# Agent attention and a squared-ReLU MLP on one core: 128- and 64-row spreads, and the weave on two engines

## The chip, the core and the metric

The kernel runs on one core of a Trainium2 chip. TensorE (PE) multiplies matrices into PSUM, VectorE (DVE), ScalarE (ACT) and GpSimd (POOL) do elementwise work, and SyncE (SP) issues the transfers, which 16 DMA engines carry out. The metric is device time in microseconds (us), the median of several runs. The profile comes from one execution of its own.

## The reference

Four batches of 12480 queries attend to 49 agents, which have attended to 12480 keys and values before. The result goes token by token through an MLP of width 2048 with a squared ReLU. All is computed to float32 accuracy.

```python
def sm(a, b):
    s = scale * (a @ b.transpose(0, 2, 1))
    e = np.exp(s - s.max(-1, keepdims=True))
    return e / (e.sum(-1, keepdims=True) + 1e-09)
agent_v = sm(agents, k) @ v          # per batch, 49 x 128
x = (sm(q, agents) @ agent_v).reshape(B * N, 128)
h = np.maximum(x @ w_in, 0.0)
out = (h * h) @ w_out
```

## The kernel before

The kernel never forms x. It folds `agent_v @ w_in` into one 49-row weight per batch (`w_hi` and `w_lo`, a high and a low part in the type fp32r), so that the first MLP matmul takes the 49 softmax probabilities of a token as its input. For accuracy the probabilities too are split in two parts, high and low.

**Steps.** The 49920 tokens are cut into tiles of 512, and the 2048 hidden columns into 8 pairs of 128. A step is one tile and one pair: `mm1` (L432, 6 matmuls into `h`), `relu` on ScalarE (L438), and for two steps together `square` on ScalarE (L441), `high` (L445) and `low` (L449) on VectorE, which make `gh` and `gl`. Five steps later (`LAG`) `mm2` (L460, 12 matmuls) takes them into an output pair, which `store` sends out every eighth step. A block s is 1024 tokens, 16 steps; there are 48.75 blocks. PSUM holds two `h` tiles.

**Probabilities of a block.** `mm1` reads block s from two tiles: `p_a` has the high parts in partitions 0 to 48 and the low parts in 64 to 112, `p_b` the other way round. For blocks 0 to 2 they are made with matmuls. For s > 2 the way is this: scores (L179), `q_shift`, `q_exp`, `q_inverse`, then `q_norm` on GpSimd (L349), `q_hi` on ScalarE (L353), `q_lo` on GpSimd (L356). `q_words` (L375, GpSimd, two calls) takes the 32-bit parts apart into 16-bit words in the single tile `words`, whose columns 49 to 63 and 113 to 127 stay zero. `q_turn` (L380, SyncE) transposes `words` into `turned` with a DMA. `q_weave` (L384, ScalarE) puts lower and upper 16-bit words together again in `woven`, a full tile of 128 partitions. `q_spread` (L391, SyncE) copies `woven` into `p_b` in two transfers of 49 rows, halves exchanged, and into `p_a` in one of 113 rows (`AW` = 64 + 49). A row is 1024 float32 values, 4 KB.

**Batch work.** For batches 1 to 3 keys and values are loaded in 13 pieces each (`kt`, `vt`; L174, L221), scored (L179), reduced, made into exponentials (`sk`; GpSimd L214, ScalarE L217) and multiplied with v (L229), woven in between the steps of the batch before.

**What sets the order.** The program is written out by hand in an order that a planner makes: `at(t, f)` gives a function a place in units of steps, and `chain` finds free places on the engines with the distances of the table `hop` (two steps from GpSimd or PE to ScalarE, for instance). Each engine goes through its own instructions in this order. Loads of `kt`, `vt` and `qt` stand 5 steps ahead of their matmuls. All transfers go through SyncE's one queue, so one that waits holds up the next. `plan_tokens` sets the turn 1.9 steps after the words, the weave 5 steps (and the half of a place that `chain` adds) after them, and the spread 0.9 steps after the weave, at least 3 steps before the block's first `mm1`:

```python
at(end + 1.9, q_turn, s)
_, end = chain(end + 5, [("ACT", q_weave, s)])
at(end + .9, q_spread, s)
```

Of the kernel before, what the change touches and what calls it, by code (L numbers as in the profile page):

```python
# [13 lines left out]
U16 = mybir.dt.uint16  # L14
# [4 lines left out]
P = 128  # L19
CH = 120  # L20
G = 8
# [4 lines left out]
def agent_attention_relu2_kernel(ctx: ExitStack, tc: tile.TileContext, qT, kT, v, agT, w_in, w_out, outT):  # L26
# [6 lines left out]
    nc = tc.nc  # L33
# [10 lines left out]
    AW = L + A  # L44
    rg = (slice(0, L), slice(L, P))
# [6 lines left out]
    ra = (slice(0, A), slice(L, AW))  # L52
# [3 lines left out]
    io = ctx.enter_context(tc.tile_pool(name="io", bufs=9))  # L56
# [98 lines left out]
    kts, vts, pss = {}, {}, {}  # L155
# [150 lines left out]
    PT, qs, es, sms, pps = {}, {}, {}, {}, {}  # L306
# [72 lines left out]
        pss["t", s] = io.tile([P, 2 * G, P], U16, name="turned", tag="io")  # L379
        nc.sync.dma_start(out=pss["t", s], in_=words.rearrange("p c w n -> p (c w n)"), transpose=True)  # L380

    def q_weave(s):
        PT["x"] = io.tile([P, G, P, 2], U16, name="woven", tag="io")
        nc.scalar.copy(PT["x"].rearrange("p c n w -> p c w n"), pss.pop(("t", s)).rearrange("p (c w) n -> p c w n", w=2))  # L384

    def q_spread(s):
        if s > 2:
            x = PT.pop("x").rearrange("p c n w -> p (c n w)").bitcast(F32).rearrange("p (c n) -> p c n", n=P)
            pa, pb = PT[s] = (wk.tile([P, G, P], F32R, name="p_a"), wk.tile([P, G, P], F32R, name="p_b"))
            for to, src in ((pb[ra[0]], x[ra[1]]), (pb[ra[1]], x[ra[0]]), (pa[:AW], x[:AW])):  # L390
                nc.sync.dma_start(out=to.bitcast(F32), in_=src)  # L391
            return
        pa, pb = PT[s]
        x = PT.pop("x") if s == 0 else None
        todo = ((pa[ra[0]], x[ra[0]]), (pb[ra[1]], x[ra[0]]), (pa[ra[1]], x[A:2 * A]), (pb[ra[0]], x[A:2 * A])) if s == 0 else (
            (pb[ra[0]], pa[A:2 * A]), (pb[ra[1]], pa[ra[0]]), (pa[ra[1]], pb[ra[0]]))
        for to, src in todo:
            nc.sync.dma_start(out=to.bitcast(F32), in_=src.bitcast(F32))
# [74 lines left out]
    def at(t, f, *args):  # L473
        steps.append((t, len(steps), f, args))
# [11 lines left out]
    def chain(t, todo):  # L486

        first = prev = None  # L490
        while todo:
            n = 1
            while todo[0][0] == "PE" and n < len(todo) and todo[n][1] in reads_bank and todo[n][0] != "PE":
                n += 1
            t += hop[prev][todo[0][0]] if prev else 0
            while True:
                g, p, ts = t, None, []
                for e, *_ in todo[:n]:
                    g += hop[p][e] if p else 0
                    while (e, g) in taken or (e == "PE" and g not in slots):  # L500
                        if p == "PE" and e == "DVE":
                            break
                        g += 1
                    ts.append(g)
                    p = e
                if todo[0][0] != "PE" or ts[-1] <= ts[0] + 1:
                    break
                t += 1
            for (e, f, *args), g in zip(todo, ts):
                soon = e == "DVE" and prev == "PE"  # L510
                if soon:
                    read.add(g)
                else:
                    taken.add((e, g))
                at(g + (.49 if soon and f is q_shift else .47 if soon else .45 if e == "PE" else .5), f, *args)
                prev = e
            first = ts[0] if first is None else first
            t, todo = ts[-1], todo[n:]
        return first, t
# [3 lines left out]
    def plan_tokens(s, base):  # L523
        todo = [("ACT", q_exp, s), ("DVE", q_inverse, s), ("POOL", q_norm, s), ("ACT", q_hi, s)]
        todo += [("POOL", q_lo, s), ("PE", q_transpose, s), ("ACT", q_copy, s)] if s < 3 else [
            ("POOL", q_words, s, 0), ("POOL", q_lo, s), ("POOL", q_words, s, 1)]
        if s > 1 and s % 2 == 0:
            m = min(2, NSG - s)
            first, base = chain(base, [("PE", q_scores, s, m), ("DVE", q_shift, s, m)])
            for x in range(s, s + m):  # L530
                at(first - 5, q_load, x)
            base += 3
        _, end = chain(base, todo)
        if s > 2:
            at(end + 1.9, q_turn, s)
            _, end = chain(end + 5, [("ACT", q_weave, s)])
        at(end + .9, q_spread, s)
        assert end + 3 < s * NF, (s, end)

    def plan_batch(b, base):  # L540

        end = b * N // TT * NJ
        for n in range(0, NS, 2):
            m = min(2, NS - n)
            first, t = chain(base + int(n * 4.6), [("PE", k_scores, b, n, m), ("ACT", k_copy, n, m), ("DVE", k_pmax, n, m)])
            for x in range(n, n + m):
                if b > 1 or x:
                    at(max(base - (6 if b > 1 else 0), first - 5), k_load, b, x)
            if n == NS - 3:
                chain(t + 1, [("DVE", k_max, 0, NS - 1)])  # L550
        _, t0 = chain(t + 1, [("DVE", k_max, 1)])
        _, t0 = chain(t0 + 4, [("PE", k_max, 2), ("DVE", k_max, 3)])
        _, t0 = chain(t0 + 3, [("PE", k_max, 4), ("DVE", k_max, 5)])
        done, d = {}, (end - 31 - t0) / NS
        for n in range(NS):
            _, done[n] = chain(t0 + 1 + int(n * d), [("POOL", k_sub, n), ("ACT", k_exp, n)])
            if n:
                _, y = chain(done[n] + 1, [("DVE", e_sum, n)])
            if n == NS - 1:
                _, y = chain(y + 1, [("DVE", a_last, 0)])  # L560
            if n % 2 or n == NS - 1:
                x = n - n % 2
                first, t = chain(done[n] + 2 if n % 2 else y + 4, [("PE", v_acc, x, n + 1 - x), ("DVE", v_sum, x)])
                for y in range(x, n + 1):
                    at(first - 5, v_load, b, y)
        at(first + .46, a_last, 1)
        at(t + .475, a_last, 2)
        _, e = chain(t + 2, [("PE", w_make_all, b, 0), ("ACT", w_make_all, b, 1), ("DVE", w_make_all, b, 2)])
        assert e + 2 < end, (e, end)
        return t + 1  # L570
# [29 lines left out]
    for n in range(NS):  # L600
        t = Z + 6.3 + 2.07 * n
# [38 lines left out]
    at(t0 + 9.7, q_copy, 0)  # L640
    at(t0 + 9.74, q_load, 1)
    at(t0 + 9.75, q_spread, 0)
    at(t0 + 9.76, hold, 0)
    at(t0 + 9.77, k_load, 1, 0)
    t = t0 + 13.4
# [22 lines left out]
    for y, x in enumerate((1.15, 1.16, 1.17)):  # L668
        at(x, w_first, 0, 4, 4, y, nc.vector)
    at(3.1, warm_rows, 6)  # L670
    plan_tokens(1, 3)
    for s in range(2, NSG):
        plan_tokens(s, (s - 2) * NF + NF // 2 + LAG - (3 if s > 2 and s % 2 == 0 else 0))
    t = 0
    for b in range(1, B):
        t = plan_batch(b, t)
# [41 lines left out]
```

## Time and profile before

| | us |
|---|---|
| median of 3 runs (2337.61 to 2344.29) | 2340.14 |
| the profiled execution | 2340.53 |
| its span, first to last instruction | 2338.8 |
| PE busy | 1929.4 |
| ACT busy | 1733.2 |
| DVE busy | 1640.9 |
| POOL busy | 327.4 |

Busy times of an engine leave out the time in which it waits. A busy PE need not run at full speed: the granted clock has two levels, 2.4 GHz (1.00) and 1.2 GHz (0.50), and a stretch shows a mean of them. The DMA share is the mean over the 16 DMA engines. A wait is put down to what ended last before it.

### The profile page before, as it was taken

Reading aid. Unit: us, or ns where it says so; the run is one execution under the profiler, and the core shown is the slowest. Engines: PE = TensorE matmul, PEld = TensorE weight load, DVE = VectorE, ACT = ScalarE, POOL = GpSimd, SP = SyncE. Lnnn points to the kernel's source line nnn. Section 1 sums busy time; section 2 is a strip of 40 time slices with the busy share of each in tenths; the row PEclk is TensorE's granted clock in tenths of the full one; section 3 lists DMA queues with packets and bytes.
Section 4 is the critical chain, followed back from the end, with each engine's and each line's share of the span. In section 5 each row is a group of like instructions: output and inputs, shape, how many; then the busy total and the mean of one; then the engine's idle time right before and its main releaser. Section 6 shows DMA issues by size and latency. Waiting matters only on the chain.

```text
span 2338.8 us, 51487 instructions
## 1 busy us (share of the span) xinstructions
PE 1929.4 (82%) x23244; PEld 1588.4 (68%) x23244; DVE 1640.9 (70%) x1274; ACT 1733.2 (74%) x1535; POOL 327.4 (14%) x244
## 2 busy tenths in 40 slices
PE   9998878788877788788886878879787887888788
PEld 7776766676756666577675766667666776676676
DVE  7886767776776677757676667767667677677676
ACT  5886777787766777778776777768776877787786
POOL 1111222111012121110101220111101101101100
PEclk9998999899988889989998899989889999899899
DMA  8231222322221222222231222212211211121110
GB/s 341 100 107 37 84 79 72 97 66 94 88 75 54 61 75 88 70 81 66 92 98 59 59 55 82 91 61 66 86 41 57 59 49 62 43 64 62 44 52 27
DMA packets 144298, 177.78 MB, mean 76 GB/s; under 512 B 100602, under 2 KB 100858, under 8 KB 144078
## 3 DMA queue, kind: packets, MB, share of 16 engines
q1 hardware_dynamic: 144078, 174.48, 24.3%
q8 instruction: 182, 2.98, 0.5%
q14 instruction: 38, 0.31, 0.0%
HBM read 83.02 MB, written 25.56 MB: 46 GB/s over the span
## 4 chain that ended last, share of the span: by engine, by line
DMA 45%; PE 35%; ACT 10%; issue 4%; SPq 4%; DVE 1%; POOL 1%; ACTq 0%; DVEq 0%
DMA p_a<-woven 30%; PE pair L460 19%; PE h L432 13%; DMA kt<-kT 7%; DMA vt<-v 7%; ACT woven L384 5%; ACT rg L438 4%; SPq L391 3%; PE pair L179 1%; PE pair L229 1%; ACT rg L441 1%; POOL words L375 0%; DMA raw<-w_in 0%; ACT ob L465 0%; PE pair L238 0%
## 5 line engine op out<-in xcount | busy, mean ns | idle before, releaser
L438 ACT ACTIVATE rg<-h 128x1024 f32<-128x1024 f32 (+1 forms) x784 | 790.1, 1020 | 561.9 <-PE h L432 560.6
L449 DVE TENSOR_TENSOR gl<-rg,gh 128x2048 fp32r<-128x2048 f32 x392 | 922.3, 2353 | 19.3 <-DVE gh L445 0.5
L445 DVE CAST gh<-rg 128x2048 fp32r<-128x2048 f32 x392 | 490.4, 1251 | 435.7 <-ACT rg L441 265.5
L441 ACT ACTIVATE rg<-rg 128x2048 f32<-128x2048 f32 x392 | 749.4, 1912 | 7.9
L432 PE MATMUL h<-p_a,w_hi 49*128 49x512 f32 (+4 forms) x1616 | 544.6, 413 | 247.8 <-DMA p_a<-woven 223.7
L460 PE MATMUL pair<-gh,wo_hi 64*128 64x512 f32 x3136 | 655.1, 403 | 0.2 <-issue 0.2
L460 PE MATMUL pair<-gh,wo_lo 64*128 64x512 f32 x3136 | 653.7, 402 | 0.1
L432 PE MATMUL h<-p_b,w_hi 49*128 49x512 f32 (+4 forms) x1616 | 529.4, 414 | 1.0 <-DMA p_b<-w_lo 1.0
L432 PEld LDWEIGHTS h<-p_a,w_hi 49*128 49x128 f32 x1616 | 303.5, 196 | 308.4 <-issue 237.3
L460 PE MATMUL pair<-gl,wo_hi 64*128 64x512 f32 x3136 | 509.2, 396 | 1.3 <-DVE gl L449 1.3
L460 PEld LDWEIGHTS pair<-gh,wo_lo 64*128 64x128 f32 x3136 | 328.2, 193 | 67.2 <-issue 0.8
L460 PEld LDWEIGHTS pair<-gh,wo_hi 64*128 64x128 f32 x3136 | 328.8, 194 | 61.3 <-issue 0.6
L460 PEld LDWEIGHTS pair<-gl,wo_hi 64*128 64x128 f32 x3136 | 319.3, 190 | 60.7 <-DVE gl L449 3.0
L432 PE MATMUL h<-p_a,w_lo 49*128 49x512 f32 (+4 forms) x808 | 326.0, 403 | 0.3 <-issue 0.3
L432 PE MATMUL h<-p_b,w_lo 49*128 49x512 f32 (+4 forms) x808 | 326.1, 404 | 0.0
L432 PEld LDWEIGHTS h<-p_b,w_hi 49*128 49x128 f32 x1616 | 298.8, 196 | 25.2 <-DMA p_b<-w_lo 1.3
L349 POOL TENSOR_TENSOR e<-e,sm 128x392 f32<-128x392 f32 x48 | 79.1, 1648 | 1342.5 <-DVE sm L346 1312.2
L375 POOL COPY words<-pp 128x784 uint16<-128x784 uint16 x92 | 123.6, 1343 | 524.9 <-ACT pp L353 522.0
L432 PEld LDWEIGHTS h<-p_a,w_lo 49*128 49x128 f32 x808 | 157.2, 194 | 25.8
L432 PEld LDWEIGHTS h<-p_b,w_lo 49*128 49x128 f32 x808 | 157.1, 194 | 5.7 <-issue 0.5
L384 ACT COPY woven<-turned 128x2048 uint16<-128x2048 uint16 x46 | 116.0, 2522 | 0.0
L229 PE MATMUL pair<-sk,vt 120*32 120x49 f32 x2496 | 41.2, 235 | 78.2 <-DMA vt<-v 78.2
(108 smaller groups left out, 884.8 us busy)
## 6 DMA issues: line engine op xcount, KB each, us to landing
vt<-v SPq DMA_DIRECT2D x52, 516.0 KB
qt<-qT SPq DMA_DIRECT2D x49, 512.0 KB
kt<-kT SPq DMA_DIRECT2D x52, 480.0 KB
outT<-ob SPq DMA_DIRECT2D x97, 256.0 KB
p_a<-woven SPq DMA_DIRECT2D x46, 452.0 KB
p_b<-woven SPq DMA_DIRECT2D x92, 196.0 KB
raw<-w_in SPq DMA_DIRECT2D x4, 512.0 KB
raw<-w_out SPq DMA_DIRECT2D x4, 512.0 KB
```

What stands on the lines that cost most here:

```text
L179: nc.tensor.matmul(ps[r, u, c * A:(c + 1) * A], x[:, c, r], ag_sb[:, batch(c, r), :], start=True, stop=True)
L229: nc.tensor.matmul(ps[r], vt[:CH, c, r], piece(x)[:, c, :], start=x == n and c == 0, stop=x == n + m - 1 and c == G - 1)
L349: eng.tensor_tensor(out=es[s], in0=es[s], in1=sms.pop(s).to_broadcast([P, G, A]), op=ALU.mult)
L375: nc.gpsimd.tensor_copy(words[:, :, :, x * L:x * L + A], src)
L384: nc.scalar.copy(PT["x"].rearrange("p c n w -> p c w n"), pss.pop(("t", s)).rearrange("p (c w) n -> p c w n", w=2))
L391: nc.sync.dma_start(out=to.bitcast(F32), in_=src)
L432: nc.tensor.matmul(h[:, u, x0:x1], w[ra[u], j, :], pt[u ^ lo][ra[u], x0:x1], start=x == 0, stop=x == 2)
L438: nc.scalar.activation(rgs[p][:, x], hs.pop(i)[:, :, :width(i)], AF.Relu)
L441: nc.scalar.activation(rgs[p], rgs[p], AF.Square)
L445: nc.vector.tensor_copy(ghs[p], rgs[p])
L449: nc.vector.tensor_tensor(out=gls[p], in0=rgs.pop(p), in1=ghs[p].bitcast(F32), op=ALU.subtract)
L460: nc.tensor.matmul(outs[t][u][:, :width(i)], w[rg[u], 2 * j + e, :], g[rg[u], e, :], start=j == 0 and x == 0, stop=j == NJ - 1 and x == 5)
```

## The change

`q_weave` is cut in two. ScalarE writes the upper words (w = 1) at the place where it wrote both, and GpSimd the lower ones (w = 0), 0.6 steps later in the plan. Both write into the same 32-bit cells of `woven`. `q_spread` copies whole halves, with the zero rows 49 to 63 and 113 to 127: `p_b` in two transfers of 64 rows and `p_a` in one of 128.

```diff
-    def q_weave(s):
-        PT["x"] = io.tile([P, G, P, 2], U16, name="woven", tag="io")
-        nc.scalar.copy(PT["x"].rearrange("p c n w -> p c w n"), pss.pop(("t", s)).rearrange("p (c w) n -> p c w n", w=2))
+    def q_weave(s, w, copy):
+        if w:
+            PT["x"] = io.tile([P, G, P, 2], U16, name="woven", tag="io")
+        copy(PT["x"][:, :, :, w], pss["t", s].rearrange("p (c w) n -> p c w n", w=2)[:, :, w])
...
-            for to, src in ((pb[ra[0]], x[ra[1]]), (pb[ra[1]], x[ra[0]]), (pa[:AW], x[:AW])):
+            for to, src in ((pb[rg[0]], x[rg[1]]), (pb[rg[1]], x[rg[0]]), (pa, x)):
                 nc.sync.dma_start(out=to.bitcast(F32), in_=src)
...
-            _, end = chain(end + 5, [("ACT", q_weave, s)])
+            _, end = chain(end + 5, [("ACT", q_weave, s, 1, nc.scalar.copy)])
+            at(end + .6, q_weave, s, 0, nc.gpsimd.tensor_copy)
```

GpSimd's queue in batch 1, where `sk` subtractions stand between two blocks' probabilities (`e` is the normalisation of the next block, `pp` the low part). Before:

```order
L375 COPY words<-pp 128x16x49
L356 TENSOR_TENSOR pp<-e,pp 128x8x49
L375 COPY words<-pp 128x16x49
L214 TENSOR_TENSOR sk<-sk,mM 120x392 x2
L349 TENSOR_TENSOR e<-e,sm 128x392
```

And now:

```order
L375 COPY words<-pp 128x16x49
L356 TENSOR_TENSOR pp<-e,pp 128x8x49
L375 COPY words<-pp 128x16x49
L214 TENSOR_TENSOR sk<-sk,mM 120x392
L385 COPY woven<-turned 128x1024
L214 TENSOR_TENSOR sk<-sk,mM 120x392
L349 TENSOR_TENSOR e<-e,sm 128x392
```

The new copy stands between two subtractions; without batch work it stands right behind the second `words` copy. It waits for the transposed rows, and nothing else on this engine has moved.

SyncE's queue at the fourth and fifth turned block, with `kt` loads and an output store behind a spread. Before:

```order
L391 DMA p_a<-woven 113x1024
L174 DMA kt<-kT 128x960 x2
L467 DMA outT<-ob 128x512
L174 DMA kt<-kT 128x960
L380 DMA_TRANSPOSE turned<-words 128x16x128
L467 DMA outT<-ob 128x512
L391 DMA p_b<-woven 49x1024 x2
L391 DMA p_a<-woven 113x1024
```

And now (one line lower in the file from the weave on):

```order
L392 DMA p_a<-woven 128x1024
L174 DMA kt<-kT 128x960 x2
L468 DMA outT<-ob 128x512
L174 DMA kt<-kT 128x960
L380 DMA_TRANSPOSE turned<-words 128x16x128
L468 DMA outT<-ob 128x512
L392 DMA p_b<-woven 64x1024 x2
L392 DMA p_a<-woven 128x1024
```

The order is the same; the spreads have more rows, and the first of each three now waits for GpSimd as well as for ScalarE.

## Rows read from the trace of the kernel before

**Rows 1.** Head of the page: span, busy us of each engine with share and instructions

```profile
span 2338.8 us, 51487 instructions
PE 1929.4 (82%) x23244; PEld 1588.4 (68%) x23244; DVE 1640.9 (70%) x1274; ACT 1733.2 (74%) x1535; POOL 327.4 (14%) x244
```

**Rows 2.** Waits of PE: who for whom, us in total, times, longest

```profile
PE h L432 <- DMA p_a<-woven: 223.7, 32, 8.7
PE pair L229 <- DMA vt<-v: 78.2, 7, 12.2
PE pair L179 <- DMA kt<-kT: 71.3, 7, 11.3
PE h L432 <- ACT rg L438: 22.5, 35, 1.0
```

**Rows 3.** Timeline of SP in a block without batch work: start, us, what

```profile
2137.13 1.45 SPq L313 DMA_DIRECT2D qt<-qT  x2
...
2143.51 1.53 SPq L391 DMA_DIRECT2D p_b<-woven  x2
2145.08 0.65 SPq L391 DMA_DIRECT2D p_a<-woven  x1
```

**Rows 4.** Timeline of PE at that block's first step; idle time before in brackets

```profile
2166.99 0.76 PE L432 MATMUL h<-p_a,w_hi 49*128 49x512 f32 x1 [6.23 <-DMA p_a<-woven]
...
2170.93 0.40 PE L432 MATMUL h<-p_a,w_hi 49*128 49x512 f32 x1
...
2173.02 0.39 PE L432 MATMUL h<-p_a,w_hi 49*128 49x512 f32 x1
```

**Rows 5.** Stretches: length; busy PE, PEld, DVE, ACT, POOL; clock, DMA share, GB/s

```profile
2150.00:2157.00 7.00, 7.00 (x68) 5.73 (x62) 6.79 (x7) 5.95 (x7) 0.00 (x0) 1.00 0.07 27
2138.00:2142.00 4.00, 4.00 (x38) 3.57 (x36) 3.97 (x3) 3.76 (x4) 0.00 (x0) 1.00 0.78 278
96.60:136.60 40.00, 40.00 (x696) 32.98 (x694) 35.53 (x28) 35.13 (x36) 5.65 (x3) 1.00 0.25 82
2141.00:2185.40 44.40, 37.53 (x419) 30.71 (x417) 32.15 (x24) 34.57 (x31) 4.27 (x4) 0.92 0.18 53
```

**Rows 6.** Timeline of PE: key scores after a wait, and without one

```profile
1237.14 2.84 PE L179 MATMUL pair<-ag_sb,kt 128*32 128x49 f32 x128 [10.36 <-DMA kt<-kT]
...
1243.25 0.39 PE L432 MATMUL h<-p_a,w_hi 49*128 49x512 f32 x1
...
1143.96 1.59 PE L179 MATMUL pair<-ag_sb,kt 128*32 128x49 f32 x128
```

**Rows 7.** Page, groups of instructions: count, busy us, mean ns, idle before

```profile
L384 ACT COPY woven<-turned 128x2048 uint16<-128x2048 uint16 x46 | 116.0, 2522 | 0.0
```

**Rows 8.** Instructions on `words`: ns min/median/max, first and last start, form

```profile
L375 POOL COPY words<-pp x92: 854/858/2923, 138.1 to 2260.8; 128x784 uint16<-128x784 uint16 x92
```

**Rows 9.** Timeline of POOL in a block with batch work

```profile
1391.10 2.91 POOL L375 COPY words<-pp 128x784 uint16<-128x784 uint16 x1 [16.82 <-ACT pp L353]
...
1396.05 2.80 POOL L375 COPY words<-pp 128x784 uint16<-128x784 uint16 x1
```

**Rows 10.** Timeline of SP in the same block

```profile
1398.88 1.80 SPq L380 DMA_TRANSPOSE turned<-words  x1
...
1408.97 0.65 SPq L391 DMA_DIRECT2D p_a<-woven  x1
1409.68 7.63 SPq L221 DMA_DIRECT2D vt<-v  x1
```

**Rows 11.** Timeline of ACT in the same block: the weave

```profile
1404.84 2.54 ACT L384 COPY woven<-turned 128x2048 uint16<-128x2048 uint16 x1
```

**Rows 12.** Timeline of DVE in the same block: two subtractions

```profile
1391.00 2.29 DVE L449 TENSOR_TENSOR gl<-rg,gh 128x2048 fp32r<-128x2048 f32 x1
...
1395.27 2.86 DVE L449 TENSOR_TENSOR gl<-rg,gh 128x2048 fp32r<-128x2048 f32 x1
```

## The prediction

> **What bounds the kernel now.** I read the page's head first, then who TensorE waits for, then the timelines around one such wait. TensorE is busy 1929.4 of 2338.8 us, VectorE 1640.9, ScalarE 1733.2 [rows 1]: no engine is full, so what matters is what TensorE stands still for. Its waits are nearly all transfers: 223.7 us in 32 waits for `p_a`, 78.2 in 7 for `vt`, 71.3 in 7 for `kt` [rows 2]. That is 373.2 us in 46 waits, one for each of the 46 blocks of 1024 tokens that go through the DMA turn (s = 3 to 48).
>
> One block shows how. The `p_a` spread is issued at 2145.08 [rows 3]; TensorE stops at 2160.76 and goes on at 2166.99, when it lands [rows 4]. So it is 21.9 us under way. In the middle of it (2150 to 2157) the DMA engines are 0.07 busy, which is 1.1 of 16, at 27 GB/s [rows 5]: 113 rows of 4 KB (463 kB) trickle through about one engine. Whole 128-row tiles do not: just after two `qt` loads were issued at 2137.13 [rows 3], the share is 0.78 and the rate 278 GB/s [rows 5].
>
> The `kt` and `vt` waits have the same root. At 1408.97 a `p_a` spread is issued, and the `vt` load behind it holds SyncE for 7.63 us where a spread takes 0.65 [rows 10]: the next transfer also has a share for the engine that is clogged. `kt` and `vt` loads normally have a lead of five steps before their matmuls.
>
> **Part 1, rows of 128 and 64.** The new `p_a` is 128 x 4 KB = 524 kB, `p_b` twice 262 kB. Today 463 kB at 27 GB/s are 17.1 us, so 4.8 of the 21.9 us are start, the `p_b` pieces ahead and landing. At the rate of the `qt` loads 524 kB take 1.9 us, so `p_a` lands about 1.9 + 4.8 = 6.7 us after its issue, at 2151.8 in the block above, 9 us before TensorE asks. I take the waits of all three kinds as gone: **-373.2 us**.
>
> The Trainium skill (DMA: Bandwidth & Descriptors, "Why a DMA increments its semaphore by 16 and not by 1") says that a transfer is dealt to the largest number of engines up to 16 that divides the row count: 113 is prime and gets 1, 49 gets 7, 64 and 128 get 16. The 0.07 for 113 rows agrees; no run here shows 64 rows. By that rule the serial rival below has no chance at all; I leave it a small one.
>
> **Part 2, the clock after a stop.** After a `p_a` wait TensorE starts slowly: the first step, 2166.99 to 2170.93, takes 3.94 us, the next 2.09 [rows 4], and the block's granted clock is 0.92 [rows 5], so part of it ran at the lower level of 1.2 GHz. That is 1.85 us in 32 places, 59 us. After a `kt` wait scores and one step take 6.11 us (1237.14 to 1243.25) [rows 6]; at full clock scores are 1.59 [rows 6] and a step 2.09, so 2.43 is lost, in 14 places 34 us. Without stops the clock holds: in 96.60 to 136.60, ahead of the first turned block, TensorE is busy 40.00 of 40.00 us at clock 1.00 [rows 5]. **-93 us**.
>
> **Part 3, ScalarE writes half.** The weave costs 2.52 us, 46 times, on ScalarE [rows 7]. Half the elements at the same rate are 1.26, so 58 us leave ScalarE. TensorE stands 22.5 us in 35 waits for ScalarE's relu [rows 2], 0.64 us each; a relu that comes 1.26 earlier would cover these. I take **-20 us**, bounds 0 (ScalarE stays as late since it no longer gets a pause to catch up) and -22.5.
>
> **Part 4, GpSimd writes the other half.** No GpSimd copy of 1024 elements is in the trace. The nearest is the `words` copy of 784: 0.854 us at best, 2.923 at worst [rows 8]. Times 1024/784 that is 1.12 to 3.82; strided writes may make it longer. The long ones stand beside VectorE's subtraction, 2.91 and 2.80 us [rows 9], and without pauses VectorE is seldom idle, so I take 3.7. GpSimd is 327.4 us busy [rows 1], so 46 x 3.7 = 170 us fit. In GpSimd's queue a `sk` subtraction or the next block's `e` stands behind the new copy; both are planned two steps ahead of the ScalarE work that reads them. The spread on SyncE now waits for both halves. Even if both start together, it goes 3.7 - 2.52 = 1.2 us later than now; the 9 us of slack from part 1 hide that and what is queued behind it on SyncE (`kt`, `vt`, stores, 10 us of lead). It costs nothing unless the copy passes 11 us. VectorE pays: its subtraction takes 2.86 beside a GpSimd copy and 2.29 alone [rows 12], 0.57 x 46 = 26 us of an engine with room for it.
>
> The Trainium skill (SBUF — State Buffer, "SBUF: two separate sides") speaks against this part: GpSimd and a VectorE instruction with two SBUF inputs lock each other out of a shared port for a whole instruction. The lengthened rows of both engines agree in kind, 0.57 us on VectorE in size. By the rule VectorE loses the copy's own 1.12 us, 46 x 1.12 = 52 us, and the sum stays; it only feeds rival A.
>
> **What is late next.** In a block without batch work (2141.00 to 2185.40) ScalarE is busy 34.57 us, VectorE 32.15 [rows 5]. ScalarE's share falls to 33.3. TensorE needs 16 steps of 2.09 plus half a pair of scores (0.8), 34.2 us. So TensorE binds, with ScalarE 1 us under it and VectorE 2. Such a balance leaks a little: I add 0.2 us a block, **+9 us**, bounds 0 and 92 (2 us a block, rival A).
>
> **Sum.** 2338.8 - 373.2 - 93 - 20 + 9 = 1861.6 us span. The profiled run took 2340.53, so 1.7 lie outside; its time is 0.4 us above the median shown, which changes nothing. **1863 us.** A floor, from TensorE alone: its busy time less the slow clock, 1929.4 - 93 = 1836 us [rows 1]; since the ends of matmuls are modelled and the two clock examples may be small ones, I put the low end 21 us under that, at 1815.
>
> **Rivals.**
>
> *A, the turned rows come late.* The order of work counts in steps, and the steps now pass faster. In a crowded block the second `words` copy ends at 1398.85 [rows 9], the transpose is issued at 1398.88 [rows 10], and ScalarE weaves at 1404.84 [rows 11], with no wait. When that copy is short, more is left. After the change every block is crowded, since VectorE no longer pauses. If the landing slips by 1 to 2.5 us past the weave, ScalarE stops, and with 1 us of slack a block TensorE follows. For it: the transposes take 1.80 us to issue alone. Against: even crowded blocks show no wait now. Price: 0.7 to 2.5 us x 46 = 32 to 115, so 1890 to 1970.
>
> *B, `kt` and `vt` stay late.* Their 14 waits would be their own. Then 78.2 + 71.3 + 34 = 184 come back, 2047 us. Against: the 7.63 us issue right behind `p_a`.
>
> *C, slower: 128 rows still go one by one.* If about one engine carries any SBUF-to-SBUF spread, the larger `p_a` costs 61 kB / 27 GB/s = 2.3 us more, and the GpSimd half delays it by up to 1.2; each of 46 waits grows by 2.3 to 3.5: +106 to 161 us, about 2470. It decides as soon as the share during a spread stays near 0.07. Against: whole tiles at 0.78 [rows 5], though these come from HBM.
>
> *D, nothing changes*, within 7 us: the two `p_b` pieces, and not `p_a`, would hold the engines, and as much at 64 rows as at 49. They are issued 1.57 us ahead of `p_a` [rows 3], and the 0.07 still stands 5 to 12 us later [rows 5], so hardly.
>
> **How the numbers follow.** Forecast (1815 to 1890) 0.73; A 0.17; B 0.06; C 0.02; D 0.01; below 1815 0.01. The range takes in the forecast's and the lower half of A: 1815 to 1925, about 0.81. A measurement here tells 0.3%, 7 us, from no change; faster by more than that: all but C and D, 0.97; same 0.01; slower 0.02.
>
> **What would show it.** Right: waits for `p_a` near 0; `kt` and `vt` waits below 15 us together; mean granted clock above 0.97; TensorE busy near 1830 of 1862; DMA share in the us after a spread above 0.5; weave 1.3 us on ScalarE; GpSimd's copy 1.1 to 3.8. Wrong: a wait before the weave on ScalarE (A), `vt` waits that stay (B), 0.07 during a spread (C), a GpSimd copy above 11 us.

## The result, and the profile after

| | before | after |
|---|---|---|
| median of 4 runs, us | 2339.24 (2337.61 to 2344.29) | 1851.56 (1850.60 to 1853.33) |
| ratio | | 0.7913, 95% interval 0.7899 to 0.7927 |
| profiled execution, us | 2340.53 | 1850.6 |
| its span, us | 2338.8 | 1848.8 |
| mean granted clock | 0.911 | 0.998 |

The time is 21% shorter; 1863 us had been forecast. The head of the page of after stands against [rows 1]; its last line is the granted clock in 40 slices, in tenths.

```profile
span 1848.8 us, 51605 instructions
...
PE 1826.7 (99%) x23244; PEld 1483.4 (80%) x23244; DVE 1738.5 (94%) x1274; ACT 1673.7 (91%) x1535; POOL 579.5 (31%) x290
...
PEclk9999999999999999999999999999999999999999
```

TensorE now works 99% of a span that is 490 us shorter, and no slice has a mean clock under 0.9. VectorE went from 70 to 94%: it is nearly a second bound. The waits of TensorE in after (who for whom, us in total, times, longest), against [rows 2]:

```profile
PE pair L179 <- issue: 5.0, 5, 1.7
PE pair L461 <- DVE gl L450: 4.3, 12, 0.7
PE pair L238 <- DMA vt<-v: 2.3, 4, 1.4
...
PE h L433 <- ACT rg L439: 0.6, 1, 0.6
```

The waits for the `p_a` spread, for the `kt` pieces and for the `vt` pieces at L229 are gone, all 46 of them; the 2.3 us for `vt` are an older wait in the prologue (L238). What stands first now is 5 us long.

One spread in the timeline of SP in after (start, us, what), to be read beside [rows 3], and then the stretch behind it (columns as in [rows 5]):

```profile
1688.59 1.47 SPq L313 DMA_DIRECT2D qt<-qT  x2
...
1692.85 1.11 SPq L392 DMA_DIRECT2D p_b<-woven  x2
...
1694.01 0.62 SPq L392 DMA_DIRECT2D p_a<-woven  x1
```

```profile
1694.60:1697.00 2.40, 2.40 (x24) 1.95 (x22) 2.30 (x3) 2.37 (x3) 0.00 (x0) 1.00 0.99 256
```

The DMA share is 0.99 at 256 GB/s (614 kB in 2.4 us, so the end of the `p_b` pieces is in it), where a spread of 113 rows left it at 0.07 and 27 GB/s [rows 5]. The last part of the page, in a second profile of the changed kernel, gives the median from issue to landing (the last number, us):

```profile
p_b<-woven SPq DMA_DIRECT2D x92, 256.0 KB, 3.1
p_a<-woven SPq DMA_DIRECT2D x46, 512.0 KB, 4.7
```

4.7 us in place of the 21.9 of [rows 3, 4]. The span's 490.0 us can now be taken apart by busy times and waits of TensorE; the row of other idle time is what is left over:

| | before | after | difference | said |
|---|---|---|---|---|
| waits for `p_a`, `kt`, `vt` | 373.2 | 0 | -373.2 | -373.2 |
| PE busy (the clock) | 1929.4 | 1826.7 | -102.7 | -93 |
| waits for ScalarE's relu | 22.5 | 0.6 | -21.9 | -20 |
| all other idle time of PE | 13.7 | 21.5 | +7.8 | +9 |
| span | 2338.8 | 1848.8 | -490.0 | -477 |

That the second row is the clock can be counted: TensorE is busy for 211.8 us at the lower level (0.50) in before and for 6.8 in after. Half of that is what the level costs, 105.9 and 3.4 us, and the difference of 102.5 is the row.

### The profile page after: what moved, and what is told of

Its sections match the earlier page's. It is cut to its first block, busy times and chain, and to the rows that moved or that the text cites. A ratio compares the mean times of both kernels' runs of the same rounds, so it can differ in the third digit from the quotient of the medians.

```text
span 1848.8 us, 51605 instructions
## 1 busy us (share of the span) xinstructions
PE 1826.7 (99%) x23244; PEld 1483.4 (80%) x23244; DVE 1738.5 (94%) x1274; ACT 1673.7 (91%) x1535; POOL 579.5 (31%) x290
## 4 chain that ended last, share of the span: by engine, by line
PE 73%; DVE 13%; issue 7%; ACT 4%; DMA 3%; POOL 1%; SPq 0%; DVEq 0%; ACTq 0%
PE pair L461 45%; PE h L433 23%; DVE gl L450 5%; DVE gh L446 5%; PE pair L179 3%; ACT rg L439 2%; PE pair L229 2%; ACT rg L442 1%; DMA vt<-v 1%; DMA kt<-kT 1%; DVE ob L467 1%; DVE ea L232 1%; DMA qt<-qT 1%; ACT ob L466 0%; DVE sm L341 0%
## 5 line engine op out<-in xcount | busy, mean ns | idle before, releaser
L450 DVE TENSOR_TENSOR gl<-rg,gh 128x2048 fp32r<-128x2048 f32 x392 | 976.7, 2492 | 19.3 <-DVE gh L446 0.5
L461 PE MATMUL pair<-gh,wo_lo 64*128 64x512 f32 x3136 | 631.1, 391 | 0.2
L461 PE MATMUL pair<-gh,wo_hi 64*128 64x512 f32 x3136 | 630.3, 391 | 0.5 <-DVE e L334 0.3
L446 DVE CAST gh<-rg 128x2048 fp32r<-128x2048 f32 x392 | 543.2, 1386 | 50.5 <-ACT rg L442 43.9
L433 PE MATMUL h<-p_a,w_hi 49*128 49x512 f32 (+4 forms) x1616 | 507.9, 392 | 1.5 <-ACT rg L439 0.6
L433 PE MATMUL h<-p_b,w_hi 49*128 49x512 f32 (+4 forms) x1616 | 501.5, 392 | 1.4 <-DMA p_b<-w_lo 1.4
L461 PEld LDWEIGHTS pair<-gl,wo_hi 64*128 64x128 f32 x3136 | 300.4, 184 | 76.1 <-DVE gl L450 15.9
L375 POOL COPY words<-pp 128x784 uint16<-128x784 uint16 x92 | 171.1, 1859 | 139.0 <-ACT pp L353 136.1
L385 POOL COPY woven<-turned 128x1024 uint16<-128x1024 uint16 x46 | 104.9, 2280 | 162.0 <-DMA turned<-words 111.2
L356 POOL TENSOR_TENSOR pp<-e,pp 128x392 fp32r<-128x392 f32 x48 | 120.1, 2501 | 9.9 <-ACT pp L353 9.9
```

The costliest lines, as they stand in the source:

```text
L356: eng.tensor_tensor(out=pps[s][:, :, A:], in0=es.pop(s), in1=pps[s][:, :, :A].bitcast(F32), op=ALU.subtract)
L375: nc.gpsimd.tensor_copy(words[:, :, :, x * L:x * L + A], src)
L385: copy(PT["x"][:, :, :, w], pss["t", s].rearrange("p (c w) n -> p c w n", w=2)[:, :, w])
L433: nc.tensor.matmul(h[:, u, x0:x1], w[ra[u], j, :], pt[u ^ lo][ra[u], x0:x1], start=x == 0, stop=x == 2)
L446: nc.vector.tensor_copy(ghs[p], rgs[p])
L450: nc.vector.tensor_tensor(out=gls[p], in0=rgs.pop(p), in1=ghs[p].bitcast(F32), op=ALU.subtract)
```

## The experiments

The theory: the number of rows in the `p_a` transfer decides how many DMA engines carry it, and 128 rows take the clog away; the split weave is a small gain of its own on ScalarE. Rivals: the gain comes from the shorter weave and an earlier spread; the bytes or the `p_b` pieces decide and not the row count of `p_a`; the turned rows nearly come late. Ratios are to the kernel before on the same chip; times are medians. The changed kernel ran again on two chips: once beside the runs with only the spread, with the weave earlier and with the copy made twice, and once beside the second run of 116 rows. The other differences to it are between chips, on which the kernel before took 2338.62 to 2342.41 us.

### The changed kernel again

> The changed kernel itself, beside the next three on one chip: about 1852 us, TensorE busy 1827, no wait for a transfer.

1852.24 us, ratio 0.792 (0.7909 to 0.7931). All differences to the changed kernel below are to this, but for the last study, which has its own.

### Only the spread, with the weave whole on ScalarE

```diff
-            for to, src in ((pb[ra[0]], x[ra[1]]), (pb[ra[1]], x[ra[0]]), (pa[:AW], x[:AW])):
+            for to, src in ((pb[rg[0]], x[rg[1]]), (pb[rg[1]], x[rg[0]]), (pa, x)):
```

> Transfers of 128 and 64 rows, but the weave whole on ScalarE (2.52 us). If the row counts carry the gain: all but 10 to 22 us of it, 1862 to 1874 us, with short waits of TensorE for ScalarE's relu behind the weave (up to 46 x 0.64 = 29 us). If the split weave carries a large part of the gain: well above 1900. If GpSimd's copy costs as much through VectorE as ScalarE's half gives: 1845 to 1852.

1878.08 us, ratio 0.8037 (0.8024 to 0.8050). The rows alone bring 460 of the 486 us. The head of its page, and the first of TensorE's waits:

```profile
PE 1833.5 (98%) x23244; PEld 1481.4 (79%) x23244; DVE 1694.9 (90%) x1274; ACT 1726.3 (92%) x1535; POOL 478.4 (25%) x244
```

```profile
PE h L432 <- ACT rg L438: 22.3, 33, 1.0
```

The 22.5 us of relu waits of [rows 2] are all still there. The split weave is worth 26 us, most of it these waits; 5.9 us are TensorE's busy time (1827.6 in the run beside it), for which no cause was found. The time is 4 us above what was expected. The page shows something else: VectorE and GpSimd run the same instructions as before here, and yet are busy 54.0 and 151.0 us longer than in [rows 1]. That comes back below.

### Only the weave, with 113 and 49 rows

`q_weave` in two as in the change; the spread is untouched.

```diff
...
-            _, end = chain(end + 5, [("ACT", q_weave, s)])
+            _, end = chain(end + 5, [("ACT", q_weave, s, 1, nc.scalar.copy)])
+            at(end + .6, q_weave, s, 0, nc.gpsimd.tensor_copy)
```

> The weave split over ScalarE and GpSimd, the spread as before (113 and twice 49 rows). If the spread's 22 us close a loop (a block's spread starts only so long after the last one has landed): ScalarE's half is 1.16 us shorter, the spread starts that much earlier, 46 x 1.16 = 53 us less, about 2286. If the shorter weave is hidden behind the wait: 2339.

2304.58 us, ratio 0.9843 (0.9819 to 0.9868): 35.5 us faster than before, and 452 above the changed kernel. Its waits of TensorE:

```profile
PE h L433 <- DMA p_a<-woven: 211.3, 32, 8.4
PE pair L229 <- DMA vt<-v: 76.6, 7, 12.1
PE pair L179 <- DMA kt<-kT: 69.9, 7, 12.4
```

The relu waits went (0.6 us left), 21.9 of the gain; the spread, issued about a microsecond earlier, gave back only 15.4 of the 373.2; TensorE's busy time took 4.4 us. So the rival of the earlier spread is out as the main cause. Neither of the two sizes expected was met, and why the earlier spread gave 15 us and not more isn't settled.

### `p_a` of 113 rows, `p_b` of 64

The changed kernel with

```diff
+            for to, src in ((pb[rg[0]], x[rg[1]]), (pb[rg[1]], x[rg[0]]), (pa[:AW], x[:AW])):
```

> As the changed kernel, but p_a in 113 rows (p_b stays at 64). If p_a alone is the clog: 373 us of waits and the slow clock come back, 2240 to 2290. If p_b was part of it: 2100 or less.

2268.27 us, ratio 0.9693 (0.9667 to 0.9719). TensorE's waits:

```profile
PE h L433 <- DMA p_a<-woven: 189.9, 32, 8.5
PE pair L229 <- DMA vt<-v: 71.3, 7, 11.5
PE pair L179 <- DMA kt<-kT: 61.6, 7, 10.5
```

With `p_a` alone at 113 rows 416 of the 486 us are lost. `p_b` at 64 rows is worth 36 us against the run before this one, 0.8 us a block, but only while `p_a` clogs.

### `p_a` of 128 rows, `p_b` of 49

```diff
+            for to, src in ((pb[ra[0]], x[ra[1]]), (pb[ra[1]], x[ra[0]]), (pa, x)):
```

> As the changed kernel, but p_b in two transfers of 49 rows. If p_a alone is the clog: 1852 within 8 us. If 49 rows also clog: waits for p_b of several us in each block, above 1900.

1857.15 us in two runs (1854.77 and 1859.53), ratio 0.7936 (0.7912 to 0.7960), with no wait for either tile. That is the changed kernel within what can be told; 49 rows do no harm once `p_a` is whole.

### `p_a` of 127 rows

The last row that is left out here is one of zeros, which no matmul reads.

```diff
+            for to, src in ((pb[rg[0]], x[rg[1]]), (pb[rg[1]], x[rg[0]]), (pa[:P - 1], x[:P - 1])):
```

> As the changed kernel, but p_a in 127 rows (row 127 is a zero row that no matmul reads). If the number of rows decides how many engines share a transfer, and 127, a prime, gets one: 127 x 4 KB at 27 GB/s = 19.3 us, 2.1 more than 113 rows, so 2340 to 2400 and a DMA share of 0.07 during the spread. If only the size or whole halves matter: 1852.

2363.28 us, ratio 1.0099 (1.0071 to 1.0127), so **slower than the kernel before**, by 1.0%. One row of 128 costs 511 us. Its waits, and a stretch behind a spread that was issued at 1755.38:

```profile
PE h L433 <- DMA p_a<-woven: 259.5, 32, 10.0
PE pair L229 <- DMA vt<-v: 86.1, 7, 13.8
PE pair L179 <- DMA kt<-kT: 79.1, 7, 13.2
```

```profile
1758.00:1772.00 14.00, 11.99 (x104) 9.35 (x100) 13.32 (x11) 13.71 (x12) 1.65 (x1) 1.00 0.12 43
1763.00:1766.00 3.00, 3.00 (x30) 2.42 (x28) 2.68 (x4) 3.00 (x5) 0.00 (x0) 1.00 0.06 26
```

The share is 0.12 with an output store in it (issued at 1765.60), and 0.06 at 26 GB/s, one engine of 16, in the three us before that store. The three waits are 101.9 us above those of 113 rows, 2.21 us for each of 46 blocks; 14 rows of 4 KB at the 27 GB/s of [rows 5] make 2.1. So a transfer of 127 rows goes at the speed of one of 113, and the bytes are only a slope within that. Rival C of the prediction had put one engine for 128 rows at 106 to 161 us more waits and about 2470 us. The waits come near that (101.9), the time doesn't, since the wider `p_b` and the split weave had given back 71.9 us (2340.12 to 2268.27). The Trainium skill (DMA: Bandwidth & Descriptors, "Why a DMA increments its semaphore by 16 and not by 1") gives 127 as an example of a transfer for one engine; the run agrees.

### `p_a` of 116 rows

Three rows of zeros more than 113, and twelve fewer than in the changed kernel.

```diff
+            for to, src in ((pb[rg[0]], x[rg[1]]), (pb[rg[1]], x[rg[0]]), (pa[:AW + 3], x[:AW + 3])):
```

> As the changed kernel, but p_a in 116 rows, three more than 113. 116 is 4 x 29: if a divisor of the row count sets the engines, four carry 29 rows each, 29 x 4 KB at 27 GB/s = 4.4 us, it lands 5 to 6 us ahead of need, and the time is 1852 within 8 us, DMA share about 0.25 during the spread. If anything but 128 rows is slow: about 2250 or more.

1846.39 us in two runs, ratio 0.7882 (0.7859 to 0.7904). The stretch behind a spread:

```profile
1726.00:1728.50 2.50, 2.50 (x24) 2.00 (x24) 2.50 (x2) 2.50 (x2) 0.00 (x0) 1.00 0.27 70
```

0.27 of 16 are 4.3 engines, and 116 is divided by 4 and by no larger number up to 16: the rule of the same section of the Trainium skill holds here too. No wait for `p_a`, or for `kt` and `vt` at L179 and L229, is left, so four engines are enough for this kernel. Between 113 and 116 rows the time falls by 422 us (against 2268.27), between 116 and 127 it rises by 517.

### The weave two steps earlier

The changed kernel, made to ask for the turned rows before they land, as rival A had it.

```diff
-            _, end = chain(end + 5, [("ACT", q_weave, s, 1, nc.scalar.copy)])
+            _, end = chain(end + 3, [("ACT", q_weave, s, 1, nc.scalar.copy)])
```

> Both halves of the weave two steps (4.2 us) earlier in the plan; the turned rows land 0.6 to 6.5 us, mostly 3.3, ahead of the weave now, so ScalarE must wait for them in most blocks, about 1 us and up to 3.6. Rival A's mechanism: TensorE loses nearly all of that, 20 to 100 us more, 1872 to 1950. If ScalarE's 9% of free time takes it up: within 10 us of 1852.

1902.60 us, ratio 0.8138 (0.8126 to 0.8149): 50 us slower than the changed kernel. Its waits of ScalarE and of TensorE:

```profile
ACT woven L385 <- DMA turned<-words: 64.3, 38, 4.4
...
PE h L433 <- ACT rg L439: 40.8, 33, 3.4
```

Rival A's mechanism is real, and its price (32 to 115) takes in the 50 us. What it lacked is its condition. The group of the weave in after, by line (busy, mean ns, idle before):

```profile
L385 ACT COPY woven<-turned 128x1024 uint16<-128x1024 uint16 x46 | 62.5, 1360 | 0.0
```

ScalarE never stands before a weave. GpSimd's half in after, which waits for the same rows, begins 0.1 to 5.8 us ahead of ScalarE's (median 2.9), so the rows had landed by then. The two steps, 4.2 us, are all that separates the two kernels.

### GpSimd's copy made twice

```diff
             at(end + .6, q_weave, s, 0, nc.gpsimd.tensor_copy)
+            at(end + .61, q_weave, s, 0, nc.gpsimd.tensor_copy)
```

> GpSimd makes its half of the weave twice, the second copy over the first; the spread waits for the second. If 9 us of slack cover the spread: same time within 10 us, with GpSimd busy about 105 us more and VectorE 40 to 70 us more (1740 to about 1795, 97% of the span). If VectorE, at 94%, is as good as the bound: 1875 to 1900.

1873.42 us, ratio 0.8013 (0.8002 to 0.8024): 21 us slower, just under the second of the two sizes expected. The head of its page, and the first of TensorE's waits:

```profile
PE 1835.1 (98%) x23244; PEld 1477.3 (79%) x23244; DVE 1783.5 (95%) x1274; ACT 1677.5 (90%) x1535; POOL 700.3 (37%) x336
```

```profile
PE pair L461 <- DVE gl L450: 17.8, 37, 1.1
```

No spread is waited for, so the later one is covered, as the prediction had it. But VectorE is busy 45.5 us longer (1738.0 in the run beside it), and TensorE waits 17.8 us for its subtraction in place of 5.4; 7.5 us more are TensorE's busy time. Here a GpSimd copy costs VectorE about a microsecond, and VectorE has little left to give.

### 113 rows, prepared six steps earlier

The kernel before, with more lead in place of other rows: all of the preparation of a turned block is planned six steps earlier.

```diff
-        plan_tokens(s, (s - 2) * NF + NF // 2 + LAG - (3 if s > 2 and s % 2 == 0 else 0))
+        plan_tokens(s, (s - 2) * NF + NF // 2 + LAG - (3 if s > 2 and s % 2 == 0 else 0) - (6 if s > 2 else 0))
```

> The kernel before (113 and 49 rows, weave on ScalarE) with the whole preparation of a block, turn, weave and spread, 6 steps (12.6 us) earlier in the plan. If the transfer only came too late: the p_a waits (224 us) and their slow clock (59) go, while kt and vt loads still meet the clogged engine in 14 to 25 blocks, 10 us each: 2060 to 2150. If one clogged engine holds up all: 2339. If lead is all that is needed: 1870.

2098.78 us in two runs, ratio 0.8959 (0.8933 to 0.8985): the time is in the range expected, its parts are not quite. TensorE's waits:

```profile
PE h L432 <- DMA p_a<-woven: 60.0, 18, 4.4
PE pair L229 <- DMA vt<-v: 59.8, 7, 10.8
PE pair L179 <- DMA kt<-kT: 36.0, 5, 8.7
```

Lead takes away 14 of the 32 `p_a` waits and 163.7 of their 223.7 us, where all had been expected to go. Of the 14 `kt` and `vt` waits 12 remain, 95.8 of 149.5 us: those loads stay late behind the clogged spread. So more lead treats part of it, and the clog itself has to be taken away.

### 116 rows beside 128, once more

To tell 116 rows from the changed kernel, both ran on one chip.

> The changed kernel once more, beside 116 rows on one chip: 1850 to 1854 us if the chips agree.

> p_a in 116 rows again. It read 1846.4 where the changed kernel read 1852 on another chip. If four engines for p_a leave the rest free for other transfers and that helps: 4 to 7 us under the changed kernel here too. If the chips differ: the same within 2 us.

The changed kernel 1853.06 us (1851.29 to 1853.99, ratio 0.7920), 116 rows 1847.30 (1843.11 to 1849.30, ratio 0.7892, interval 0.7880 to 0.7903). The runs of the two don't overlap: 116 rows are 5.8 us or 0.3% faster, and **the best version here**. In the two profiles 3.2 of the 4.0 us between the spans are idle time of TensorE (22.9 and 19.7). One such place in the timeline of PE, first in the changed kernel, then with 116 rows:

```profile
1630.64 1.49 PE L179 MATMUL pair<-ag_sb,qt 128*32 128x49 f32 x115
1633.11 0.37 PE L179 MATMUL pair<-ag_sb,qt 128*32 128x49 f32 x13 [0.98 <-issue]
```

```profile
1627.91 1.59 PE L179 MATMUL pair<-ag_sb,qt 128*32 128x49 f32 x128
```

The scores of a block break off for a microsecond, with nothing to wait for that the profile shows. All such breaks in scores come to 5.0, 5.3 and 5.9 us in three profiles of the changed kernel, and to 1.0 and 3.3 with 116 rows. This one follows a spread that had been issued at 1626.57. Instructions too come by DMA, as the page's list of queues in after says (packets, MB, share of 16 engines):

```profile
q8 instruction: 182, 2.98, 0.7%
```

These packets of 16 KB could stand behind a spread that fills all 16 engines and not behind one on four. That is argued and not shown, and two runs speak against it: with 128 rows the kernel with only the spread has 1.8 us of such breaks, and the one with the earlier weave 1.1. Why 116 rows are faster stays open.

## Why the prediction was right, and where its sizes were off

**Part 1, the waits.** Right as it stood. The one example block with its 0.07 had named the cause, and 127, 116 and 113 rows show that it is the row count. The landing was forecast at 6.7 us and took 4.7; the 4.8 us of start and pieces ahead, taken from the slow spread, were too many. Nothing hung on it, since no wait for `p_a` is left.

**Part 2, the clock.** Mis-sized by a tenth: -93 said, -102.7 measured. The prediction took its 1.85 and 2.43 us from one `p_a` and one `kt` wait; over 46 places it was 2.23 each, if all of it is put to them. The mechanism held: 102.5 us of it are the lower clock's, as counted above. The low end of the range had been set below the floor for this reason.

**Part 3, ScalarE.** Right: -20 said, -21.9 measured, and the kernel with only the spread shows these waits come back when the weave is whole. ScalarE is busy 59.5 us less (58 said).

**Part 4, GpSimd's copy.** Inside its bounds of 1.12 to 3.82 us, but the value taken was too high: 3.7 said, 2.28 measured. The group on the page of after (busy, mean ns, idle before it):

```profile
L385 POOL COPY woven<-turned 128x1024 uint16<-128x1024 uint16 x46 | 104.9, 2280 | 162.0 <-DMA turned<-words 111.2
```

The shortest is 1.36 us, the longest 3.52. And it doesn't delay the spread by the 1.2 us that were said, since it starts at the landing of the turned rows and not with ScalarE's half: in the timeline of POOL and of ACT in after

```profile
1688.99 2.59 POOL L385 COPY woven<-turned 128x1024 uint16<-128x1024 uint16 x1 [4.69 <-DMA turned<-words]
...
1691.43 1.36 ACT L385 COPY woven<-turned 128x1024 uint16<-128x1024 uint16 x1
```

it ends at 1691.58, before ScalarE is done, and the spread's first piece goes at 1692.85, 1.4 us after the weave began. It is so in 45 of the 46 blocks; the median from ScalarE's weave to the spread is 1.43 us, in before 2.55. The prediction put the two halves side by side, where the queue of GpSimd had let the one go ahead.

**Part 4, what VectorE pays.** The term that failed most: 26 us said, 97.6 measured (1640.9 to 1738.5). It cost nothing in the sum, since TensorE still binds, but it is why the copy made twice cost 21 us. And VectorE is now nearer to the bound than ScalarE (1738.5 and 1673.7 us), which the prediction had the other way round. One thing was misread and two were left out.

The misreading is that of the two subtractions, 2.86 us "beside a GpSimd copy" and 2.29 "alone" [rows 12]. The one at 1391.00 was not alone: GpSimd's copy of 1391.10 to 1394.01 [rows 9] stands beside it. It had only begun first. The one at 1395.27 began while GpSimd was at the low part, until 1395.98:

```profile
1393.97 2.01 POOL L356 TENSOR_TENSOR pp<-e,pp 128x392 fp32r<-128x392 f32 x1
```

So 0.57 us is not the price of a copy. It goes with the 0.71 us that an earlier GpSimd instruction still had to run.

First of what was left out, the cast. The prediction priced the lengthened subtraction alone. By line, VectorE's two large groups on the page of before, then of after:

```profile
L449 DVE TENSOR_TENSOR gl<-rg,gh 128x2048 fp32r<-128x2048 f32 x392 | 922.3, 2353 | 19.3 <-DVE gh L445 0.5
...
L445 DVE CAST gh<-rg 128x2048 fp32r<-128x2048 f32 x392 | 490.4, 1251 | 435.7 <-ACT rg L441 265.5
```

```profile
L450 DVE TENSOR_TENSOR gl<-rg,gh 128x2048 fp32r<-128x2048 f32 x392 | 976.7, 2492 | 19.3 <-DVE gh L446 0.5
...
L446 DVE CAST gh<-rg 128x2048 fp32r<-128x2048 f32 x392 | 543.2, 1386 | 50.5 <-ACT rg L442 43.9
```

The subtraction gained 54.4 us and the cast 52.8 (their records overlap a little, so together this is more than VectorE's 97.6). The timeline of DVE beside the copy of above shows how:

```profile
1688.09 2.28 DVE L450 TENSOR_TENSOR gl<-rg,gh 128x2048 fp32r<-128x2048 f32 x1
1690.29 2.37 DVE L446 CAST gh<-rg 128x2048 fp32r<-128x2048 f32 x1
1692.70 2.29 DVE L450 TENSOR_TENSOR gl<-rg,gh 128x2048 fp32r<-128x2048 f32 x1
1694.91 1.22 DVE L446 CAST gh<-rg 128x2048 fp32r<-128x2048 f32 x1
```

The copy starts at 1688.99 during a subtraction and ends at 1691.58, 1.2 us after that one's end, not far from the 1.36 us of the shortest copies. The cast that begins at 1690.29 takes 2.37 us where the next one takes 1.22. It goes by who begins first, as a count over the whole trace of after shows. The 35 subtractions that were running when a GpSimd instruction began took 2.28 us (median), and 156 that began while one was running 2.81; for the casts it is 1.18 (92) and 1.98 (99).

Second, the older work. The idle times at the ends of the two cast rows say that VectorE stood 435.7 us before casts, and now 50.5. While it paused, GpSimd ran alone; now they nearly always meet: 66 of the 92 `words` copies took under 0.9 us in before, and 6 in after. Subtractions and casts that began while a GpSimd instruction was running went from 95 to 255. The kernel with only the spread has no copy on GpSimd and has 54.0 of the 97.6 us; the copy itself adds 43.6, or 0.95 us each. With only the weave, where the pauses stay, the copy adds 25.4 (1666.3 to 1640.9). That this is the 26 of the prediction is luck: the subtraction, which the term priced, gained 11.4 us (922.3 to 933.7), and the cast, which it left out, 14.4 (490.4 to 504.8). The Trainium skill (SBUF — State Buffer, "SBUF: two separate sides") says that of a GpSimd instruction and one of VectorE with two SBUF inputs the one that starts first holds the shared port to its end; the counts above agree in kind. The prediction's estimate by that rule, 52 us, is nearer to the copy's 43.6 than its own 26.

**What is late next.** TensorE binds with 99%, and its other idle time grew by 7.8 us (+9 said). That the two agree is in part luck: the term was for an engine that binds nearly as much, and TensorE's wait for VectorE's subtraction grew by 3.0 us only, from 1.3 to 4.3. The breaks in scores grew by 4.5, to 5.0. The rows of before:

```profile
PE pair L460 <- DVE gl L449: 1.3, 4, 0.4
PE pair L179 <- issue: 0.5, 1, 0.5
```

**The rivals.** A did not come in, and the weave two steps earlier shows that it would have cost some 50 us. B fell with the `kt` and `vt` rows: their lateness had the spread's root. C fell with the share of 0.99, D with the first number.

## What to carry to other kernels

Where a transfer is under way far longer than its bytes explain, look at the DMA share behind its issue: 0.07 of 16 is one engine, and a few rows of zeros more, up to a count that a large number (16 at most) divides, by the section of the Trainium skill cited above, may be worth hundreds of microseconds. When a stall is removed, price what two engines take from each other in the kernel without the stall; a mean over a kernel with pauses is too low. Before a duration is called alone, look at what the other engine was running when it began. An edit on an engine that does not bind still needs its margin named: here two steps before the weave and a microsecond on VectorE each decided over 20 to 50 us.

## What the runs showed of the hardware

One row of 128 decided over 511 us (127 rows, 2363.28), and three rows over 422 (113 to 116). A clogged spread holds later transfers too: the longest issue of a `vt` load was 8.14 us with 113 rows, 9.85 with 127, 3.16 with 116 and 1.34 with 128. A cast with one input, 1.22 us alone, took 2.37 where it began during a GpSimd copy, and casts that began first took 1.18 (median); the prediction had counted only the subtraction with its two inputs. And the widest spread isn't the best one: with a share of 0.27 the kernel was 5.8 us faster than with 0.99, for a cause that isn't shown.
